# Two of eight experts multiplied in plain float32 in place of three split products

## The chip, the cores and the metric

The kernel runs on one core of a Trainium2 chip. The metric is the device time of one launch in microseconds. The median of three runs of the kernel before is 1239.47 us (1236.13 to 1243.42).

## The reference

Three stages follow one another: an attention over 4 x 12 heads of 448 tokens with 64 columns; a mixture of 8 experts over the 1792 tokens of 768 columns that come out of it, each token going to exactly one expert and each expert taking 224 tokens; and a dense layer with 2048 hidden columns.

```python
def _moe_ref(x, w_gate, w1, w2):
    logits = x @ w_gate
    order = np.argsort(-logits.flatten())
    for idx in order:                      # best (token, expert) pair first
        tok, e = idx // E, idx % E
        if assigned[tok] >= 0 or counts[e] >= cap: continue
        assigned[tok] = e; counts[e] += 1
    for e in range(E):
        mask = assigned == e
        h = np.maximum(x[mask] @ w1[e], 0.0)     # 224 x 768 by 768 x 1024
        out[mask] = h @ w2[e]                    # 224 x 1024 by 1024 x 768
def _moe2_ref(x, w_in, w_out):
    h = x @ w_in
    g = h * (1.0 / (1.0 + np.exp(-1.702 * h)))
    return g @ w_out
```

## The kernel before

After the attention (up to about 350 us of the span) the class `Moe` takes the experts in the order in which they fill up, two at a time (a pair): expert 0, expert 1, then the dense layer for their 448 tokens, and so on for four pairs. Weights come in chunks: an expert has 8 chunks of `w1` (768 x 128, 384 KB) and 6 of `w2` (1024 x 128, 512 KB), a pair of the dense layer 28 chunks.

A float32 product is made of three products in the reduced type `float32r`. `split` turns a chunk's tile `raw` into a high part `whi` (ScalarE, L966) and a low part `wlo` = raw - whi (L969: GpSimd for expert 0, in turn with VectorE for the later experts, by LO_VECTOR). The tokens are split in the same way: `xs` (L1022 and L1023), the hidden `hs` (L1061 and L1064), the output `zs` (L1061 and L1066). `mm3` (L1030 to L1032) then issues three products for each block of 128 x 128 weights: high by high, high by low, low by high. A block of an expert has 224 moving columns, one of the dense layer 448. A `w1` chunk has 6 blocks (18 products), a `w2` chunk 8 (24 products).

`ahead` keeps the chunks coming: up to 4 chunks loaded ahead and 2 split ahead. A `raw` buffer (there are 4) is free as soon as both parts are written.

`manual_schedule` leaves the instructions of each engine in the order in which the code issues them. After each chunk `back` issues other work with a budget: steps of the routing (`Route`), which finds the tokens of the next expert, and steps of `Convert`, which rewrites the dense layer's weights. The routing of expert 1 stands among the chunks of expert 0: 32 rank compares on VectorE (L568, L570, L574) write `B` and `Bd`, of which 8 and 16 buffers exist, and after each four of them TensorE sums them up (L591, L597) between two chunks; then come the counts (L605), a decision, sixteen one-hot rows `O` on VectorE (L642) with their products (L649), and the gather of expert 1's tokens by two GpSimd DMAs (L1007). During expert 1, GpSimd issues sixteen scatter DMAs (L694, tile `left`) that pack the remaining tokens; the routing of expert 2 starts on them. `Convert` steps run on ScalarE and VectorE (L886, L887, L900, L905), with loads `r` and stores `din` and `dout` on SyncE's queue, where the weight loads (L957) stand too.

Of the kernel before, what the change touches and what calls it, by code (L numbers as in the profile page):

```python
# [20 lines left out]
FT = mybir.dt.float32  # L21
# [4 lines left out]
AF = mybir.ActivationFunctionType  # L26
# [6 lines left out]
BESIDE = [3, 5, [(48, 1), (48, 3)]]  # L33
LO_VECTOR = [(0, 2, 4, 6, 8, 10, 12), (1, 3, 5, 7, 8, 11, 13)]
IDLE = (2, 4, 5)
GATE_A = (0, 4)
GATE_B = (2, 6)
PREP_AHEAD = (6, 5, 4, 2)
# [12 lines left out]
class Attn:  # L51
# [319 lines left out]
    def run(s, slot, beside):  # L371
# [27 lines left out]
        def gates(h, f, at):  # L399
            b, gs = divmod(h - 12, 12)  # L400
            for half in range(2):
                if b >= 0 and gs == at[half]:
                    f(b, half)
# [9 lines left out]
        for i in range(4):  # L413
# [7 lines left out]
            XP=lambda h: pairs(h, 5) and h < NHD - (5 < 7) and s.put_x((h - 5) // 2),  # L421
            GA=lambda h: gates(h, s.gate_a, GATE_A), GB=lambda h: gates(h, s.gate_b, GATE_B))
        for h in range(NHD):
# [496 lines left out]
class Moe:  # L920
# [20 lines left out]
    def load(s, n):  # L941
        kind, e, i = s.chunks[n]
        if kind in ("w1", "w2") and e not in s.reg:
            s.reg[e] = s.nc.sync.value_load(s.r.eid[0:1, e:e + 1], min_val=0, max_val=7)
        K = 6 if kind == "w1" or (kind == "w32" and i < 16) else 8
        t = s.pw.tile([128, 8, 128], FT, name="raw", bufs=4)[:, 0:K]
        if kind == "w32":
# [9 lines left out]
        s.nc.sync.dma_start(t, src)  # L957
        s.raw[n] = t

    def split(s, n):  # L960
        nc = s.nc
        t = s.raw.pop(n)
        K = t.shape[1]
        hi = s.pw.tile([128, 8, 128], FR, name="whi", bufs=3)[:, 0:K]
        lo = s.pw.tile([128, 8, 128], FR, name="wlo", bufs=3)[:, 0:K]
        nc.scalar.copy(hi, t)  # L966
        kind, e, i = s.chunks[n]
        eng = nc.vector if kind != "w32" and e > 0 and i + 8 * (kind == "w2") in LO_VECTOR[e % 2] else nc.gpsimd
        f = lambda: eng.tensor_tensor(lo, t, hi.bitcast(FT), op=OP.subtract)  # L969
        if eng is nc.vector:  # L970
            s.late[n] = f
        else:
            f()
        s.hl[n] = (hi, lo)

    def ahead(s):
        N = len(s.chunks)
        while s.nl < N and s.nl < s.used + s.LOAD:
            kind, e, _ = s.chunks[s.nl]
            if kind != "w32" and not s.r.done[e]:  # L980
                break
            if s.nl >= s.nsp + 4:
                break
            s.load(s.nl)
            s.nl += 1
        while s.nsp < s.nl and s.nsp < s.used + s.SPLIT:
            s.split(s.nsp)
            s.nsp += 1
# [23 lines left out]
    def xsplit(s, e, d):  # L1012

        nc = s.nc
        if d == 0:
            s.xs = s.pa.tile([128, 6, 2, 224], FR, name="xs", bufs=1)
        p = s.ps.tile([128, 2, 2, 112], FT, name="tr", bufs=2)
        for dd in range(2):
            for c in range(2):
                nc.tensor.transpose(p[:, dd, c], s.xg[:, c, (d + dd) * 128:(d + dd + 1) * 128], s.identf)  # L1020
        p = p.rearrange("p d c t -> p d (c t)")
        nc.scalar.copy(s.xs[:, d:d + 2, 0, :], p)  # L1022
        s.ev.append(lambda xs=s.xs: nc.vector.tensor_tensor(  # L1023
            xs[:, d:d + 2, 1, :], p, xs[:, d:d + 2, 0, :].bitcast(FT), op=OP.subtract))
# [9 lines left out]
    def expert(s, e, zs):  # L1034
        nc = s.nc
        s.low()
        xs = s.xs
        hs = s.pa.tile([128, 16, 2, 448], FR, name="gs", bufs=1)[:, 0:4].rearrange("p f h t -> p (f h t)")
        hs = hs.rearrange("p (f h t) -> p f h t", h=2, t=224)
        for f in range(8):  # L1040
            w = s.weights()
            p = s.ps.tile([128, 448], FT, name="mm", bufs=3)[:, 0:224]
            for d in range(6):
                s.mm3(p, w, d, (xs[:, d, 0], xs[:, d, 1]), d == 0, d == 5)
            s.ev.append(lambda f=f, p=p: s.parts(p, hs[:, f], AF.Relu))
            yield
        s.low()
        o = (e % 2) * 224
        for d in range(6):
            w = s.weights()  # L1050
            p = s.ps.tile([128, 448], FT, name="mm", bufs=3)[:, 0:224]
            for f in range(8):
                s.mm3(p, w, f, (hs[:, f, 0], hs[:, f, 1]), f == 0, f == 7)
            s.ev.append(lambda d=d, p=p: s.parts(p, zs[:, d, :, o:o + 224], AF.Copy))
            yield
        s.low()
# [116 lines left out]
    def run(s):  # L1173
# [13 lines left out]
        for pr in range(4):  # L1187
            zs = s.pa.tile([128, 6, 2, 448], FR, name="zs", bufs=1)
            for e in (2 * pr, 2 * pr + 1):
                early, done = None, 0  # L1190
                for n, _ in enumerate(s.expert(e, zs)):
# [11 lines left out]
                    if e == 0 and s.r.done[1]:  # L1203
# [3 lines left out]
                        elif n > early + 1 and done < 6:  # L1207
                            s.xsplit(1, done)
                            done += 2
                    s.back(0 if n == 7 else (3.1 if e == 0 else 1.4 if e == 1 else 0.6 if n < 8 else 1.2), True if e > 1 and n % 2 == 1 else None, e in IDLE and (e % 2 == 1 or bool(s.r.done[e + 1])))  # L1210
                if e == 0:
# [110 lines left out]
```

## Time and profile before

| | |
|---|---|
| median of three runs | 1239.47 us |
| the profiled execution | 1235.44 us, its span 1233.7 us |
| TensorE busy | 1147.0 us (93%) |
| VectorE, ScalarE, GpSimd busy | 768.1, 649.8, 695.6 us |
| first product of expert 0 | 376.87 us |
| first product of expert 1 | 444.71 us |
| first product of the dense layer, pair 0 | 494.07 us |

An engine's busy time includes the time in which an instruction has begun and waits for a memory port. A matmul's end is modelled, so the distance between the starts of two matmuls tells more than their durations. The granted clock of TensorE is given as a share of 2.4 GHz: 1.0 or 0.5 at a moment, and a mean over a stretch.

### The profile page before, as it was taken

What the parts mean: (1) busy time and instruction counts of PE and PEld (TensorE: products, weight loads), DVE (VectorE), ACT (ScalarE), POOL (GpSimd) and SP (SyncE); (2) the same over time, 40 slices, a digit from 0 to 9 for tenths busy, and PEclk for the clock granted to TensorE, in tenths of its full rate; (3) what the DMA queues carried; (4) which work ended last, traced back from release to release, by engine and by line L of the source; (5) the groups of instructions that cost most, each with busy time, mean ns of one, the idle gap of its engine ahead of it and who ended that gap; (6) DMA issues with size and microseconds to landing.
All of it is one profiled execution on the core that took longest, in us unless ns stands there. A gap on an engine that the chain in (4) does not pass through costs nothing.

```text
span 1233.7 us, 20534 instructions
## 1 busy us (share of the span) xinstructions
PE 1147.0 (93%) x7624; PEld 984.6 (80%) x7624; DVE 768.1 (62%) x1427; ACT 649.8 (53%) x1289; POOL 695.6 (56%) x591
## 2 busy tenths in 40 slices
PE   4899999999966887999999999999999999999995
PEld 3677767777535787888899988898998999999995
DVE  7699999999779766999754466455347303331100
ACT  4798889888642244765334454224544324444420
POOL 2688778883444476544645945545544565445552
PEclk9799999999957799999999999999999999999998
DMA  6455454523134277797647633437743345653421
GB/s 163 124 136 135 123 163 121 150 76 92 26 87 113 65 206 206 223 285 232 184 134 196 179 105 115 125 97 203 201 119 110 112 131 161 179 176 106 137 80 34
DMA packets 185508, 173.02 MB, mean 140 GB/s; under 512 B 9536, under 2 KB 159808, under 8 KB 185408
## 3 DMA queue, kind: packets, MB, share of 16 engines
q1 hardware_dynamic: 180080, 160.55, 45.6%
q0 software_dynamic: 4224, 11.14, 3.1%
q8 instruction: 60, 0.98, 0.3%
q14 instruction: 40, 0.33, 0.1%
q10 hardware_dynamic: 1104, 0.03, 0.1%
HBM read 147.96 MB, written 23.72 MB: 139 GB/s over the span
## 4 chain that ended last, share of the span: by engine, by line
PE 48%; DVE 8%; POOL 3%; DMA 2%; issue 1%; ACT 1%; POOLq 0%; ACTq 0%
PE mm L1030 15%; PE mm L1031 15%; PE mm L1032 15%; DMA xg<-xd,idx 2%; DVE B L568 2%; DVE B L570 1%; DVE wc L900 1%; DVE Bd L574 1%; POOL left L694 1%; PE tr L1099 1%; POOL wlo L969 1%; DVE wc L905 1%; PE tr L1020 1%; DVE gs L1078 1%; PE rc L591 1%
## 5 line engine op out<-in xcount | busy, mean ns | idle before, releaser
L969 POOL TENSOR_TENSOR wlo<-raw,whi 128x768 fp32r<-128x768 f32 (+1 forms) x175 | 371.0, 2122 | 369.6 <-ACT whi L966 358.9
L966 ACT CAST whi<-raw 128x768 fp32r<-128x768 f32 (+1 forms) x224 | 207.9, 928 | 181.4 <-issue 74.9
L1030 PE MATMUL mm<-gs,whi 128*128 128x224 f32 (+1 forms) x768 | 253.1, 330 | 1.2 <-DVE zs L1066 1.2
L1032 PE MATMUL mm<-gs,wlo 128*128 128x224 f32 (+1 forms) x768 | 248.7, 324 | 4.3 <-POOL wlo L969 4.3
L1031 PE MATMUL mm<-gs,whi 128*128 128x224 f32 (+1 forms) x768 | 248.7, 324 | 0.0
L1032 PEld LDWEIGHTS mm<-gs,wlo 128*128 128x128 f32 x768 | 148.5, 193 | 11.1 <-POOL wlo L969 4.8
L1030 PEld LDWEIGHTS mm<-gs,whi 128*128 128x128 f32 x768 | 148.6, 193 | 8.9 <-issue 1.5
L1031 PEld LDWEIGHTS mm<-gs,whi 128*128 128x128 f32 x768 | 148.6, 193 | 5.6
L1030 PE MATMUL mm<-zs,whi 128*128 128x448 f32 x384 | 143.6, 374 | 0.2 <-DVE zs L1066 0.2
L1032 PE MATMUL mm<-zs,wlo 128*128 128x448 f32 x384 | 141.1, 367 | 0.0
L1031 PE MATMUL mm<-zs,whi 128*128 128x448 f32 x384 | 141.0, 367 | 0.0
L239 ACT ACTIVATE A<-S,sm 112x448 f32<-112x448 f32 x192 | 122.6, 658 | 6.6 <-DVE sm L232 6.5
L232 DVE TENSOR_REDUCE sm<-S 112x2 f32<-112x896 f32 x96 | 104.2, 1086 | 21.2 <-PE S L221 20.1
L1030 PE MATMUL mm<-xs,whi 128*128 128x224 f32 x384 | 111.2, 290 | 6.1 <-DVE gs L1064 6.1
L1032 PE MATMUL mm<-xs,wlo 128*128 128x224 f32 x384 | 108.9, 284 | 4.2 <-POOL rspace L693 4.2
L1031 PE MATMUL mm<-xs,whi 128*128 128x224 f32 x384 | 109.7, 286 | 1.2 <-DVE xs L1023 1.1
L248 PE MATMUL pA<-ident,A 112*112 112x112 f32 x768 | 100.9, 266 | 2.5 <-DVE AT L257 2.2
L248 PEld LDWEIGHTS pA<-ident,A 112*112 112x112 f32 x768 | 84.9, 137 | 14.8 <-DVE AT L257 3.5
L969 DVE TENSOR_TENSOR wlo<-raw,whi 128x768 fp32r<-128x768 f32 (+1 forms) x49 | 61.1, 1246 | 55.3 <-ACT whi L966 55.2
L1076 ACT ACTIVATE mm<-mm 128x448 f32<-128x448 f32 x64 | 33.8, 528 | 113.0 <-PE mm L1032 113.0
L1030 PEld LDWEIGHTS mm<-xs,whi 128*128 128x128 f32 x384 | 77.5, 202 | 10.5 <-DVE gs L1064 7.6
L221 PE MATMUL S<-khi,qT 128*112 128x448 f32 x192 | 80.8, 421 | 4.4 <-ACT khi L209 4.4
(216 smaller groups left out, 2315.7 us busy)
## 6 DMA issues: line engine op xcount, KB each, us to landing
raw<-in_moe_w_dram SPq DMA_DIRECT2D x64, 384.0 KB
raw<-in_moe_w_dram SPq DMA_DIRECT2D x48, 512.0 KB
raw<-din SPq DMA_DIRECT2D x64, 384.0 KB
raw<-dout SPq DMA_DIRECT2D x48, 512.0 KB
r<-in_moe_w_in_dram SPq DMA_DIRECT2D x24, 512.0 KB
r<-in_moe_w_out_dram SPq DMA_DIRECT2D x24, 512.0 KB
din<-wc SPq DMA_DIRECT2D x24, 256.0 KB
dout<-wc SPq DMA_DIRECT2D x48, 128.0 KB
```

Source lines behind the costliest of these rows:

```text
L221: nc.tensor.matmul(p[:, c, 0:448], s.qT[h][:, i, :], mv.rearrange("p i t -> p (i t)"), start=(n == 0), stop=(n == 1))
L232: s.nc.vector.tensor_reduce(s.sums[h][:, 2 * u:2 * u + 2, 0], s.Sp[u][:, :, 0:448], axis=AX.X, op=OP.max, negate=True)
L239: s.nc.scalar.activation(s.A[h][:, i, :], p[:, c, 0:448], AF.Exp, bias=sm[:, i, 0:1], scale=1.0, accum_out=sm[:, i, 1:2])
L248: nc.tensor.transpose(p[:, qc], s.A[h][:, qc, kc * 112:(kc + 1) * 112], s.identf)
L568: V.tensor_scalar(b[:, 0:k], src[:, 0:k], sv, None, op0=OP.is_lt)
L570: V.tensor_scalar(b[:, k:], src[:, k:], sv, None, op0=OP.is_le)
L966: nc.scalar.copy(hi, t)
L969: f = lambda: eng.tensor_tensor(lo, t, hi.bitcast(FT), op=OP.subtract)
L1030: nc.tensor.matmul(p, hi[:, k], x[0], start=first, stop=False)
L1031: nc.tensor.matmul(p, hi[:, k], x[1], start=False, stop=False)
L1032: nc.tensor.matmul(p, lo[:, k], x[0], start=False, stop=last)
L1076: nc.scalar.activation(p, p, AF.Gelu_apprx_sigmoid)
```

## The change

For the experts in `FULL` (0 and 1) nothing is split. The loaded tile `raw` is itself the stationary operand, `xs` and `hs` are copied once in full float32, and one float32 product stands where three stood. The output `zs` is split as before, since the dense layer keeps its three products. As TensorE now reads `raw` itself, a buffer is free when the chunk's last product has run, and `ahead` loads one chunk less ahead while the chunk in use is such a one.

```diff
+FULL = (0, 1)
...
+    def whole(s, n):
+        kind, e, _ = s.chunks[n]
+        return kind != "w32" and e in FULL
...
     def split(s, n):
         t = s.raw.pop(n)
+        if s.whole(n):
+            s.hl[n] = t
+            return
...
-        while s.nl < N and s.nl < s.used + s.LOAD:
+        while s.nl < N and s.nl < s.used + s.LOAD - (s.used > 0 and s.whole(s.used - 1)):
...
+        if e in FULL:
+            nc.scalar.copy(s.xs[:, d:d + 2, 0, :].bitcast(FT), p)
+            return
         nc.scalar.copy(s.xs[:, d:d + 2, 0, :], p)
...
-                s.mm3(p, w, d, (xs[:, d, 0], xs[:, d, 1]), d == 0, d == 5)
-            s.ev.append(lambda f=f, p=p: s.parts(p, hs[:, f], AF.Relu))
+                if e in FULL:
+                    nc.tensor.matmul(p, w[:, d], xs[:, d, 0].bitcast(FT), start=d == 0, stop=d == 5)
+                else:
+                    s.mm3(p, w, d, (xs[:, d, 0], xs[:, d, 1]), d == 0, d == 5)
+            if e in FULL:
+                s.ev.append(lambda f=f, p=p: nc.scalar.activation(hs[:, f, 0].bitcast(FT), p, AF.Relu))
+            else:
+                s.ev.append(lambda f=f, p=p: s.parts(p, hs[:, f], AF.Relu))
...
-                s.mm3(p, w, f, (hs[:, f, 0], hs[:, f, 1]), f == 0, f == 7)
+                if e in FULL:
+                    nc.tensor.matmul(p, w[:, f], hs[:, f, 0].bitcast(FT), start=f == 0, stop=f == 7)
+                else:
+                    s.mm3(p, w, f, (hs[:, f, 0], hs[:, f, 1]), f == 0, f == 7)
```

On GpSimd's queue at the start of expert 1 there stand before the change, between the gather of its tokens (`xg`) and the scatter (`left`), low parts of weights:

```order
L1007 DMA xg<-xd,idx 112x768 x2
L969 TENSOR_TENSOR wlo<-raw,whi 128x1024
L969 TENSOR_TENSOR wlo<-raw,whi 128x768
L693 MEMSET rspace 1x1
L694 DMA left_157<-rec_68,pos 3584x10
```

and after it, from the last scatter to the next low part, which is the dense layer's:

```order
L694 MEMSET rspace 1x1
L695 DMA left_157<-rec_68,pos 3584x10
L978 TENSOR_TENSOR wlo<-raw,whi 128x768 x16
L978 TENSOR_TENSOR wlo<-raw,whi 128x1024 x7
L1016 DMA xg<-xd,idx 112x768 x2
```

The 28 low parts of experts 0 and 1 that stood on GpSimd and VectorE are gone, and the sixteen scatters follow one another.

On SyncE's queue, where the loads of expert 0 end, there stand before the change (`eid` is the number of the expert, `din` a store and `r` a load of `Convert`):

```order
L957 DMA raw<-in_moe_w_dram 128x8x128
L944 TENSOR_LOAD eid
L944 ISA x2
L957 ISA
L957 DMA raw<-in_moe_w_dram 128x6x128
L870 DMA din<-wc 128x4x128
L862 DMA r_5406<-in_moe_w_out_dram 128x2x512
```

and after it:

```order
L958 DMA raw<-in_moe_w_dram 128x8x128
L871 DMA din<-wc 128x4x128
L863 DMA r_5188<-in_moe_w_out_dram 128x2x512
L945 TENSOR_LOAD eid
L945 ISA x2
L958 ISA
L958 DMA raw<-in_moe_w_dram 128x6x128
```

The first load of expert 1 moved behind one store and one load of `Convert`.

## Rows read from the trace of the kernel before

**Rows 1.** Busy time by stretch; us, then each engine, clock, DMA share, GB/s.
```profile
377.00:441.00 64.00, 51.47 (x401) 45.85 (x400) 51.53 (x116) 18.31 (x31) 30.04 (x17) 0.79 0.35 100
441.00:494.00 53.00, 42.91 (x349) 41.12 (x347) 36.87 (x60) 25.37 (x47) 36.03 (x39) 0.94 0.71 202
500.00:560.00 60.00, 57.55 (x322) 50.10 (x321) 58.00 (x105) 41.54 (x72) 26.77 (x14) 0.97 0.85 265
```

**Rows 2.** Timeline of TensorE, stations: start us, us, line, tiles, idle before.
```profile
376.87 0.54 PE L1030 MATMUL mm<-xs,whi 128*128 128x224 f32 x1
...
389.95 0.27 PE L1032 MATMUL mm<-xs,wlo 128*128 128x224 f32 x1
...
390.71 0.37 PE L1030 MATMUL mm<-xs,whi 128*128 128x224 f32 x1
...
412.54 0.54 PE L591 MATMUL rc<-B,Cp 112*32 112x448 f16 x5 [0.98 <-DVE B L568]
...
414.34 0.53 PE L1030 MATMUL mm<-xs,whi 128*128 128x224 f32 x1
...
444.71 0.35 PE L1030 MATMUL mm<-xs,whi 128*128 128x224 f32 x1
...
474.68 0.37 PE L1032 MATMUL mm<-gs,wlo 128*128 128x224 f32 x1 [3.57 <-POOL wlo L969]
...
494.07 0.47 PE L1030 MATMUL mm<-zs,whi 128*128 128x448 f32 x1 [0.21 <-DVE zs L1066]
```

**Rows 3.** Timeline of VectorE and GpSimd during the routing of expert 1.
```profile
360.77 3.09 DVE L642 TENSOR_SCALAR O<-iota,acc 112x224 f16<-112x224 f16 x16
...
367.79 3.58 POOL L969 TENSOR_TENSOR wlo<-raw,whi 128x768 fp32r<-128x768 f32 x2
...
369.22 2.23 DVE L568 TENSOR_SCALAR B<-vr,v 112x112 f16<-112x112 f32 x1 [2.27 <-ACT vr L549]
...
386.11 4.25 DVE L568 TENSOR_SCALAR B<-vr,v 112x896 f16<-112x896 f32 x7
...
401.25 0.26 DVE L568 TENSOR_SCALAR B<-vr,v 112x112 f16<-112x112 f32 x1
...
402.22 0.33 DVE L568 TENSOR_SCALAR B<-vr,v 112x224 f16<-112x224 f32 x1
...
423.46 7.18 DVE L642 TENSOR_SCALAR O<-iota,acc 112x224 f16<-112x224 f16 x16
```

**Rows 4.** Timeline of TensorE, split products of expert 0, at two clocks.
```profile
431.66 0.41 PE L1030 MATMUL mm<-gs,whi 128*128 128x224 f32 x1
431.87 0.41 PE L1031 MATMUL mm<-gs,whi 128*128 128x224 f32 x1
...
434.16 0.27 PE L1030 MATMUL mm<-gs,whi 128*128 128x224 f32 x1
...
437.73 0.27 PE L1032 MATMUL mm<-gs,wlo 128*128 128x224 f32 x1
```

**Rows 5.** Timeline of TensorE, plain float32 products of the attention, 448 columns.
```profile
49.49 0.55 PE L268 MATMUL av<-AT,vt 112*64 112x448 f32 x2
49.87 0.55 PE L268 MATMUL av<-AT,vt 112*64 112x448 f32 x2
50.24 0.55 PE L268 MATMUL av<-AT,vt 112*64 112x448 f32 x2
```

**Rows 6.** Timeline of ScalarE before the first compare.
```profile
367.87 0.83 ACT L966 CAST whi<-raw 128x768 fp32r<-128x768 f32 x1 [1.43 <-DMA raw<-in_moe_w_dram]
368.60 0.53 ACT L549 COPY vr<-rv 112x448 f32<-112x448 f32 x1
```

**Rows 7.** Expert 1: SyncE's weight loads, a ScalarE wait for one, and DMA share.
```profile
450.63 6.63 SPq L957 DMA_DIRECT2D raw<-in_moe_w_dram  x3
...
455.56 0.83 ACT L966 CAST whi<-raw 128x768 fp32r<-128x768 f32 x1 [2.69 <-DMA raw<-in_moe_w_dram]
...
460.00:470.00 10.00, 8.67 (x71) 8.49 (x71) 4.44 (x7) 5.63 (x10) 8.76 (x13) 0.93 0.91 250
```

## The prediction

> **What bounds the kernel now.** I read the busy times by stretch first. The change touches only 377 to 494 us, the experts 0 and 1. There TensorE is busy for 51.47 of 64 and 42.91 of 53 us, at a mean clock of 0.79 and 0.94 [rows 1]. The next stretch, the dense layer of pair 0, has TensorE busy for 57.55 of 60 us at 0.97: it is bound by TensorE, and what is saved ahead of it should move it as a block. So the question is what the stretch of experts 0 and 1 waits for.
>
> Second, the pace of the products. Split products with 224 columns start 0.111 us apart at full clock (33 of them stand from 434.16 to 437.73) and 0.21 at half (431.66, 431.87) [rows 4]. The 576 products of the two experts, at 0.111, are 64 us; the stretch from the first of them to the dense layer takes 494.07 - 376.87 = 117.2 us [rows 2]. The other 53 us are the routing's own small products, waits, and half clock.
>
> Third, the waits. In expert 0 the routing on VectorE is late, since GpSimd's low parts hold it up: a compare of 112 columns that takes 0.26 us at 401.25 takes 2.23 us at 369.22, until the two low parts that began at 367.79 are through; sixteen one-hot rows take 3.09 us before any low part runs, and 7.18 us with them [rows 3]. TensorE's queue holds the rank products between the chunks, so each such stall stops it too, and after it the clock is at half. In expert 1 TensorE waits for a low part directly, for instance 3.57 us ahead of 474.68 [rows 2].
>
> **The change part by part.** *TensorE's products get dearer.* A float32 product of the attention runs as two instructions. Those on the same half of the array start at 49.49, 49.87 and 50.24, 0.375 us apart for 448 columns at full clock [rows 5]; by columns that is 0.188 us for 224, more than the 0.111 that a split product takes, load included. A block then takes 2 x 0.188 = 0.375 us where three products took 0.333. That is 0.042 more for each of 192 blocks, +8.1 us if nothing else changed. A `w1` chunk is 6 blocks = 2.25 us, a `w2` chunk 8 blocks = 3.0 us.
>
> The Trainium skill has two rules for this product. FP8 and Floating Point Precision (TensorE Precision Notes) gives true float32 four passes through the array, with which the 0.375 agrees. Perfetto Trace Analysis (Engine Utilization, first note) halves the array's output rate for FP32_LOW_HIGH, which would make it two passes; that is the third rival below.
>
> *Splits go.* 28 high parts on ScalarE, 28 low parts on GpSimd and VectorE, the low parts of `xs` and `hs`. These lie beside TensorE and count only where it waits, so I walk from station to station.
>
> Start of expert 0. The copy `vr` waited for a high part, which ended about 368.7 (367.87 + 0.83) [rows 6]; without it the compares start some 2 us sooner, and the first is not stalled for 2 us. The first product waits for the tokens, whose gather is not changed; only the low part of `xs` falls away: 376.2, estimated, for 376.87.
>
> Chunks 0 to 6. Seven chunks are 15.8 us; a first stretch at half clock costs 1.3 (my estimate); between two chunks the rank products take from 389.95 to 390.71 less one step, 0.65 us [rows 2], six times 3.9. Chunk 6 ends at 397.2. VectorE could do its 32 compares sooner, at 0.61 (4.25 / 7) for a plain one and 0.97 (401.25 to 402.22) for one with its diagonal [rows 3], but 8 buffers hold it back: the last eight, of the dearer sort, can begin after chunk 4, about 391.8, and take 7.8 us: 399.6. So TensorE still waits here, 2.4 us. The tail of the ranking with the counts was 412.54 to 414.34, 1.8 us: chunk 7 starts at 401.4 where it was 414.34, **13 us sooner** [rows 2].
>
> Rest of expert 0: one `w1` and six `w2` chunks 20.3, one-hot products 3.2 (paced by 3.09 us of VectorE), small products and transposes 1.5, and half clock after the two pauses, which I put at 3.4 (between 0 and 7). That is 28.4: expert 1 starts at 429.8 for 444.71, **15 us sooner**. A move on SyncE lies here: expert 1's first load now stands behind a store that waits for VectorE. VectorE is through with it about 418, and a load that was issued about 451 landed by 455.6 [rows 7], 5 us: 424, before 429.8. Nothing waits.
>
> Expert 1: 36.0 us of chunks, 1.2 of transposes for the routing, 1.0 of rank products. The scatter on GpSimd begins about 419 and runs without low parts between: the routing has its data before the transposes come. New here is the wait of a load for the *end* of a chunk: it has three chunks, 6.8 us, to land, against those 5. The loads of this expert, the first of the next and `Convert`'s come to about 9 MB in 37 us, 250 GB/s, what the DMA queues moved at a share of 0.91 [rows 7]. I add 3 us (0 to 7). Pair 0 starts at 429.8 + 41.2 = 471.0 for 494.07: **23 us sooner**.
>
> *Pair 0 and later.* Instructions and order are the same, TensorE is the bound, VectorE's backlog is smaller: no change.
>
> Sum: 1235.44 - 23 = 1212.4 for an execution like the profiled one (span 1233.7). The median of the runs is 4.0 above that one, so I forecast **1216 us**. The open sizes (half clock 0 to 7 for 3.4, DMA 0 to 7 for 3, the first product) make it 1209 to 1223.
>
> **The rivals.** *Loads pace expert 1.* If a load takes 9 us instead of 5 under the denser traffic, each chunk lasts 3 us and more, and expert 1 is some 10 us longer: 1226. For it speaks the share of 0.91 and the shorter lead, against it that 250 GB/s is not the most that was moved (265 over 60 us at 0.85 in rows 1).
>
> *Pair 0 gives it back.* VectorE is busy for 58.00 of 60 us there [rows 1]. If that is `Convert` pacing the dense layer's chunks, an earlier start only means waits for them, about a third of the gain: 1224. Against it: TensorE is as busy, and VectorE comes in with less left to do.
>
> *Float32 needs two passes.* Then the load of the weights is the limit, about 0.111 us an instruction, a block 0.222 us, 29 us less on TensorE for both experts. Expert 0 would wait for the compares, expert 1 for 32 us of loads; of the 29 about 17 remain: 1199. The 0.375 of rows 5 speaks against it.
>
> *Slower: the clock stays at half.* The float32 block takes 0.75 us at half clock, 0.375 more. My sum has some 4.7 us of that loss. From about 62 more blocks of the 192 on the 23 us are gone; if all of expert 0 and half of expert 1 ran so, the loss would be 54 us less 4.7 already counted: 1265. Before, half clock followed each pause of TensorE; the pauses become fewer, and the clock was full while the attention ran its float32 products at 49.49. So it is unlikely.
>
> *Nothing moves*: if the routing's chain through VectorE had its length for another reason than GpSimd. The twins in rows 3 speak against it.
>
> **How the numbers follow.** Forecast 0.70; loads 0.12; pair 0 0.07; two passes 0.04; half clock 0.04; nothing 0.03. 1216 is the likeliest case. The range 1206 to 1228 takes in its own bounds with 3 us for the spread of the runs, and the two cases in which part is given back; about 0.15 are left out. A measurement here can tell some 0.5%, 6 us, from no change: faster than 1233.3 are the forecast and nearly all of the cases with a smaller gain, 0.91; within 0.5% 0.04; slower 0.05.
>
> **What the profile after would show.** Right: two instructions to a block, 0.188 us apart; compares without 2 us stalls; chunk 7 near 401, expert 1 near 430, pair 0 near 471, and from there the same distances as before. Wrong: a step far from 0.188; TensorE idle for DMA `raw` in expert 1; pair 0 longer than before; a mean clock below 0.8 between 377 and 430.

## The result and the profile after

The changed kernel took 1219.91 us (median of 4 runs, 1217.41 to 1221.09), the kernel before beside it 1239.38 (1236.13 to 1243.42). The ratio is 0.9843, its 95% interval 0.9815 to 0.9871: 19.5 us faster. Forecast were 1216 us and 1206 to 1228. The profiled execution took 1219.52 us. Its page begins (busy us, share of the span, instructions)

```profile
span 1217.7 us, 20040 instructions
...
PE 1146.2 (94%) x7432; PEld 982.7 (81%) x7432; DVE 722.8 (59%) x1398; ACT 626.0 (51%) x1261; POOL 646.6 (53%) x570
```

TensorE is busy for as long as before (1147.0 us), VectorE and GpSimd for 45 and 49 us less. So nearly all of the 16.0 us by which the span shrank is time in which TensorE waited; the dearer products (8.1 us by the prediction's sum) and the shorter time at half clock must about cancel.

Busy time by stretch comes first (columns as in [rows 1]). The stretches are cut where expert 0, expert 1 and the dense layer of pair 0 now begin or run.

```profile
377.00:426.00 49.00, 47.87 (x336) 42.23 (x336) 28.45 (x95) 7.49 (x19) 7.15 (x14) 0.98 0.55 152
426.00:478.00 52.00, 43.47 (x219) 40.29 (x218) 15.34 (x42) 13.67 (x32) 15.05 (x23) 0.90 0.65 186
480.00:540.00 60.00, 57.54 (x307) 49.81 (x306) 56.59 (x94) 39.80 (x68) 26.84 (x14) 0.94 0.85 255
```

Expert 0 keeps TensorE busy for 47.87 of 49 us at a clock of 0.98, where it was 51.47 of 64 at 0.79 [rows 1]. Expert 1 does not look like that: 8.5 us of 52 are idle and the clock is 0.90. Pair 0 is what it was, 57.54 of 60 for 57.55.

The stations on TensorE's timeline (start, us, line, tiles, idle time before), to be laid beside [rows 2]:

```profile
375.57 4.32 PE L1057 MATMUL mm<-xs,raw 128*128 128x224 f32 x12
...
395.21 2.54 PE L1057 MATMUL mm<-xs,raw 128*128 128x224 f32 x12
...
399.89 0.54 PE L592 MATMUL rc<-B,Cp 112*32 112x448 f16 x5 [0.68 <-DVE B L569]
...
401.52 1.76 PE L1057 MATMUL mm<-xs,raw 128*128 128x224 f32 x8
...
425.94 0.94 PE L1057 MATMUL mm<-xs,raw 128*128 128x224 f32 x4
428.18 1.02 PE L1057 MATMUL mm<-xs,raw 128*128 128x224 f32 x4 [1.31 <-issue]
432.45 7.98 PE L1057 MATMUL mm<-xs,raw 128*128 128x224 f32 x28 [3.25 <-issue]
442.95 6.63 PE L1057 MATMUL mm<-xs,raw 128*128 128x224 f32 x24 [2.52 <-ACT gs L1061]
451.04 7.05 PE L1057 MATMUL mm<-xs,raw 128*128 128x224 f32 x36 [1.45 <-DMA raw<-in_moe_w_dram]
...
477.88 0.47 PE L1042 MATMUL mm<-zs,whi 128*128 128x448 f32 x1
```

Chunk 7 of expert 0 starts at 401.52 (was 414.34), expert 1 at 425.94 (444.71), pair 0 at 477.88 (494.07). So 18.8 us had been won when expert 1 began, and 16.2 when it ended: expert 1 took 51.9 us, more than the 49.4 of before. From pair 0 to the end of the span it is 739.8 us for 739.6.

VectorE's compares and one-hot rows in 377 to 441 us (line, operation, shape, count; busy us, mean ns of one; idle before):

```profile
L569 DVE TENSOR_SCALAR B<-vr,v 112x896 f16<-112x896 f32 x9 | 5.6, 682 | 5.8 <-PE rc L592 5.8
L571 DVE TENSOR_SCALAR B<-vr,v 112x896 f16<-112x896 f32 x8 | 4.9, 682 | 1.0 <-issue 0.6 <-PE rc L592 0.4
L643 DVE TENSOR_SCALAR O<-iota,acc 112x224 f16<-112x224 f16 x16 | 3.2, 272 | 0.5 <-PE rc L650 0.5
```

No compare is stalled: the widest take 0.68 us each, and the sixteen rows `O` 3.2 us, where 7.18 were needed [rows 3]. What VectorE waits for now is a free buffer `B`, that is, TensorE.

The four waits of TensorE in expert 1 were not in the forecast. ScalarE's timeline there shows what stands behind them:

```profile
427.60 0.53 ACT L1032 COPY xs<-tr 128x448 f32<-128x448 f32 x1 [4.42 <-PE tr L1029]
428.02 0.61 ACT L1082 ACTIVATE zs<-mm 128x224 fp32r<-128x224 f32 x2
431.87 0.53 ACT L1032 COPY xs<-tr 128x448 f32<-128x448 f32 x1 [3.23 <-remote]
...
442.55 0.85 ACT L1061 ACTIVATE gs<-mm 128x224 f32<-128x224 f32 x3 [9.03 <-remote]
```

The transposes that fill `tr` had all ended at 426.10. The copies of them ran at 427.60 and 431.87. The last products of chunks 0 to 2 of expert 1 ended about 434, 438 and 440 us; all three evictions ran together at 442.55. "remote" says that the trace has no instruction that ended when the awaited semaphore was counted up: the awaited one, on TensorE, had ended 2 to 8 us before. The trace also records when each semaphore was counted up: TensorE's at 427.57 and 431.85, and then not before 442.46, each time just before the copy or the evictions ran. A product's end is modelled, so it stays open whether the count alone was late or the writing of the result too. SyncE waited for the same counts, since a weight buffer is free when TensorE's last product on it is through:

```profile
425.43 17.42 SPq L958 DMA_DIRECT2D raw<-in_moe_w_dram  x2
442.89 0.54 SPq L871 DMA_DIRECT2D din<-wc  x1
```

Two loads fill 17.42 us of its queue; the second left at 442.48. All this falls together with GpSimd's sixteen scatters, most of which stand 1.25 us apart, from 419.70 to 440.04:

```profile
419.70 0.97 POOL L695 DMA_INDIRECT left<-rec,pos  x1 [4.73 <-DVE pos L689]
420.67 0.09 POOL L694 MEMSET rspace<- 1x1 f32 x1
420.97 0.95 POOL L695 DMA_INDIRECT left<-rec,pos  x1 [0.22 <-issue]
```

Two readings of this were open: the loads are too few ahead for chunks of 2.3 us, or the counts of TensorE come late beside the scatters and hold up evictions and loads alike.

### The profile page after: what moved, and what is told of

Read it like the earlier page. It is cut to its first block, busy times and chain, and to the rows that moved or that the text cites. A ratio compares the mean times of both kernels' runs of the same rounds, so it can differ in the third digit from the quotient of the medians.

```text
span 1217.7 us, 20040 instructions
## 1 busy us (share of the span) xinstructions
PE 1146.2 (94%) x7432; PEld 982.7 (81%) x7432; DVE 722.8 (59%) x1398; ACT 626.0 (51%) x1261; POOL 646.6 (53%) x570
## 4 chain that ended last, share of the span: by engine, by line
PE 78%; DVE 13%; DMA 2%; ACT 2%; issue 2%; POOL 1%; another core or an unknown queue 1%; POOLq 0%; SPq 0%; DVEq 0%; ACTq 0%
PE mm L1042 16%; PE mm L1043 15%; PE mm L1044 15%; PE S L222 7%; PE av L269 6%; PE pA L249 5%; PE mm L1072 3%; DVE wc L901 2%; PE mm L1057 2%; DMA xg<-xd,idx 2%; DVE B L569 2%; PE tp L188 1%; PE tp L203 1%; DVE B L571 1%
## 5 line engine op out<-in xcount | busy, mean ns | idle before, releaser
L978 POOL TENSOR_TENSOR wlo<-raw,whi 128x768 fp32r<-128x768 f32 (+1 forms) x154 | 324.9, 2111 | 354.5 <-ACT whi L975 351.2
L975 ACT CAST whi<-raw 128x768 fp32r<-128x768 f32 (+1 forms) x196 | 182.0, 928 | 137.0 <-issue 44.3
L1042 PE MATMUL mm<-gs,whi 128*128 128x448 f32 (+1 forms) x672 | 224.2, 334 | 0.0
L1043 PE MATMUL mm<-gs,whi 128*128 128x448 f32 (+1 forms) x672 | 220.4, 328 | 0.0
L1044 PE MATMUL mm<-gs,wlo 128*128 128x448 f32 (+1 forms) x672 | 220.3, 328 | 0.0
L1042 PEld LDWEIGHTS mm<-gs,whi 128*128 128x128 f32 x672 | 128.1, 191 | 7.4 <-issue 1.5
L1044 PEld LDWEIGHTS mm<-gs,wlo 128*128 128x128 f32 x672 | 128.2, 191 | 6.4 <-POOL wlo L978 0.2
L1043 PEld LDWEIGHTS mm<-gs,whi 128*128 128x128 f32 x672 | 128.3, 191 | 5.5
L269 PE MATMUL av<-AT,vt 112*64 112x448 f32 x384 | 82.5, 552 | 0.0
L978 DVE TENSOR_TENSOR wlo<-raw,whi 128x768 fp32r<-128x768 f32 (+1 forms) x42 | 51.2, 1219 | 50.8 <-ACT whi L975 50.8
L1042 PEld LDWEIGHTS mm<-zs,whi 128*128 128x128 f32 x384 | 73.0, 190 | 9.9 <-issue 3.8
L1099 DVE TENSOR_TENSOR gs<-mm,gs 128x448 fp32r<-128x448 f32 x64 | 39.5, 619 | 69.7 <-ACT gs L1098 69.6
L1042 PE MATMUL mm<-xs,whi 128*128 128x224 f32 x288 | 80.0, 278 | 0.9 <-DVE gs L1085 0.9
```

Of the source, the lines that this page charges most:

```text
L269: nc.tensor.matmul(p[hh * 64:(hh + 1) * 64, :], s.grp[g]["v"][:, hl, kc * 64:(kc + 1) * 64], s.AT[h][:, kc, :], start=(kc == 0), stop=(kc ...
L1042: nc.tensor.matmul(p, hi[:, k], x[0], start=first, stop=False)
L1043: nc.tensor.matmul(p, hi[:, k], x[1], start=False, stop=False)
L1044: nc.tensor.matmul(p, lo[:, k], x[0], start=False, stop=last)
L1099: s.ev.append(lambda f=f, p=p: nc.vector.tensor_tensor(gs[:, f, 1], p, gs[:, f, 0].bitcast(FT), op=OP.subtract))
```

## The experiments

**One expert at a time.** `FULL = (0, 1)` becomes `(0,)` and `(1,)`.

> Expert 0 alone in whole float32; expert 1 is split again as in the kernel before. Theory (the gain is VectorE, which GpSimd's low parts no longer stall; the loss in expert 1 is GpSimd's 16 scatters without a break, beside which TensorE's semaphore counts arrive late): expert 0 as in the changed kernel, expert 1 starts at 426, plus or minus 2; expert 1's low parts break up the scatters again, so expert 1 takes 46 to 50 us, as the 49.4 of before, pair 0 starts at 472 to 476, and the time is 1214 to 1220 us, no worse than the changed kernel. Rival (each expert saves its half by having one product in place of three): 1229 to 1231 us.

> Expert 1 alone in whole float32; expert 0 is split as in the kernel before. Theory (as for the run with expert 0 alone): expert 0 as in the kernel before, expert 1 starts at 445, plus or minus 2; expert 1 takes 48 to 53 us with the scatters in one unbroken run, so pair 0 starts at 493 to 498 and the time is 1233 to 1243 us: nothing gained. Rival (each expert saves its half): 1229 to 1231 us.

Expert 0 alone gave 1220.07 us, ratio 0.9844 (0.9804 to 0.9883); expert 1 alone 1225.01, ratio 0.9880 (0.9838 to 0.9923); before was 1237.85. The two gains, 17.8 and 12.8 us, add up to 30.6, near the 30.0 that both experts gave in the run `after_again` below. For expert 0 the time is at the top of the theory's range and expert 1 starts at 426.13 as expected, but it takes 51.3 us, not 46 to 50, and pair 0 starts at 477.40, not by 476: TensorE waits 2.0, 3.0 and 1.9 us there for GpSimd, where the low parts of expert 1 stand among the scatters. With expert 1 alone both sides missed: I had forecast nothing, the rival half of 19.5. Its 96 float32 blocks ran without a pause beside 16 scatters in one unbroken run (441.34 to 461.90):

```profile
446.88 18.34 PE L1057 MATMUL mm<-xs,raw 128*128 128x224 f32 x96
465.69 6.29 PE L1072 MATMUL mm<-gs,raw 128*128 128x224 f32 x32 [0.48 <-ACT gs L1061]
...
485.73 0.47 PE L1042 MATMUL mm<-zs,whi 128*128 128x448 f32 x1
```

Expert 1 took 38.8 us here, with the same lead of loads and the same scatters as in the trace above where it took 51.9. The short lead of loads falls as a cause by this run. The scatters alone were not enough either; no count came late in expert 1 of this trace.

**No scatters.** The sixteen scatters become one copy (the compaction is left out).

```diff
+        if n == 16:
+            nc.sync.dma_start(s.left[n2][0:112 * n2, :].rearrange("(p j) c -> p j c", j=n2), s.rec[:, 0:n2, :])
+        else:
```

> The changed kernel, with the 16 indirect stores of the first compaction of tokens replaced by one plain copy of the first 12 columns (the compaction is left out, so later experts route other tokens; shapes and all other work are the same). Theory (the scatters hold back TensorE's semaphore counts, by which evictions and weight loads start): evictions of expert 1's first chunks follow their products within 1 us, weight loads start as buffers come free, expert 1 takes 41 to 44 us in place of 51.9, pair 0 starts at 467 to 470 and the time is 1208 to 1213 us. Rival (a lead of three weight loads is too short for float32 chunks of 2.3 us, whatever GpSimd does): expert 1 still takes 49 us or more, time 1217 to 1221 us.

1214.65 us, ratio 0.9793 (0.9748 to 0.9839). The time is a little above the 1208 to 1213 expected. Expert 1 took 39.6 us and pair 0 started at 465.0, both sooner than expected, but the run does not tell the two readings apart: the session was one in which counts were in time beside unbroken scatters too (`one_alone` above, `no_low_part` below). A run without scatters in a session with late counts is lacking. The total also moved by something else. Without the scatters the routing of expert 2 is issued sooner, TensorE's queue holds its products earlier, and the first half of pair 0 (465.0 to 544.1) took 79.1 us where it takes 67 to 72 in the other runs; TensorE waited there for VectorE's compares and one-hot rows, 7.1 us in all.

**Three products, no low part.** In the kernel before, experts 0 and 1 read the high part in place of the low part, which is not made.

```diff
+        if kind != "w32" and e < 2:
+            s.hl[n] = (hi, hi)
+            return
```

> The kernel before, with three products for a block throughout, but the low parts of the weights of experts 0 and 1 are not computed: the products with the low part read the high part once more (a part of the computation of experts 0 and 1 is replaced). Theory (GpSimd's low parts stalled VectorE's compares; the number of products has little to do with the gain): expert 0's compares run unstalled, the wait after its chunk 6 ends at 399 to 403, expert 1 starts at 420 to 428 in place of 444.71; expert 1 meets the unbroken scatters and takes 45 to 53 us; time 1212 to 1222 us. Rival (the gain comes from one product in place of three): expert 1 starts after 436 and the time is 1230 us or more.

1209.49 us, ratio 0.9764 (0.9725 to 0.9803): with all three products left, the gain is there, 28.4 us. Expert 1 starts at 424.3, as the theory had it; it takes 41.2 us, not 45 to 53 (no count came late in this trace), and the time is below the 1212 to 1222 expected. So one product in place of three is not where the time goes; the absent low parts are.

**Low parts that nobody needs.** The changed kernel, with GpSimd's subtractions of before put back, into a tile that is never read.

```diff
         if s.whole(n):
             s.hl[n] = t
+            kind, e, i = s.chunks[n]
+            if not (e > 0 and i + 8 * (kind == "w2") in LO_VECTOR[e % 2]):
+                d = s.spare[:, 0:K]
+                nc.gpsimd.tensor_tensor(d, t, d, op=OP.subtract)
             return
```

> The changed kernel, with a subtraction on GpSimd for each chunk of experts 0 and 1 whose low part GpSimd made in the kernel before: same size, from the loaded weights into a spare tile that nobody reads, so nothing waits for it but the reuse of the weight buffer. Theory (GpSimd's work as such stalls VectorE's compares, and TensorE waits for these): compares that last 0.68 us stretch to 2 to 4 us again, the wait after expert 0's chunk 6 ends at 406 to 413 in place of 398.5, expert 1 starts at 433 to 445 in place of 424.6, the time is 10 to 20 us above the changed kernel's on the same chip. Rival (before, TensorE waited for the low parts themselves, not for VectorE): expert 1 starts at 424 to 427 and the time is within 3 us of the changed kernel's.

1231.73 us (10 runs), 14.1 above the changed kernel in the same session (1217.59). Expert 1 starts at 446.0, 1 us later than the top of what was expected and 20.9 later than in `after_third`, a run of the changed kernel beside it. The time grows by less, since expert 1 takes 45.1 us, without a late count, for 50.8 there. The timelines of VectorE, GpSimd and TensorE:

```profile
385.28 11.06 DVE L571 TENSOR_SCALAR B<-vr,v 112x896 f16<-112x896 f32 x8
396.27 2.36 DVE L569 TENSOR_SCALAR B<-vr,v 112x112 f16<-112x112 f32 x1
...
399.09 2.41 DVE L575 SCALAR_TENSOR_TENSOR Bd<-vr,v,before 112x112 f16<-112x112 f32 x1
```

```profile
382.15 19.22 POOL L977 TENSOR_TENSOR spare<-raw,spare 128x768 f32<-128x768 f32 x6 [8.36 <-DMA raw<-in_moe_w_dram]
```

```profile
410.13 0.91 PE L592 MATMUL rc<-B,Cp 112*32 112x448 f16 x5 [2.65 <-DVE B L569]
...
412.57 1.84 PE L1063 MATMUL mm<-xs,raw 128*128 128x224 f32 x4
```

Eight compares take 11.06 us in place of 4.9; one of 112 columns takes 2.36 us, much as the stalled one in [rows 3], while six subtractions fill GpSimd. Chunk 7 is back at 412.57. Nothing waits for these subtractions' results, and ahead of expert 1 TensorE's waits are for VectorE's compares (8.1 us) and one-hot rows (2.4), none for a load. So in expert 0 it is GpSimd's work as such, through VectorE, that held TensorE. This agrees with the Trainium skill, SBUF — State Buffer (SBUF: two separate sides), by which VectorE and GpSimd share a pair of ports that one of them holds for a whole instruction.

**The kernels once more.** No edit. A session below is a set of runs made one after the other on the same chip.

> The changed kernel as it is, once more, since in its first trace TensorE's semaphore counts arrived 2 to 8 us late beside GpSimd's scatters, while in the runs with expert 1 alone and with no low part, beside the same unbroken scatters, they did not. Theory A (late counts belong to that execution or chip): expert 1 takes 39 to 42 us, pair 0 starts at 464 to 468 in place of 477.88, the time is 1205 to 1211 us. Theory B (late counts come with the combination of both experts in float32 and the scatters): expert 1 takes 49 us or more again, and the time is 1217 to 1222 us.

> The kernel before as it is, for its trace on the chip of the other runs. Theory A: no count of TensorE's semaphore comes late beside the scatters, so the pause of 3.6 us at 471 is gone or shorter; pair 0 starts at 488 to 494. Theory B: the trace is as it was, with pair 0 at 494.

> The changed kernel as it is, a third time, to stand beside the two runs below on the same chip. Where no count of TensorE's semaphore is late: 1203 to 1209 us, expert 1 39 to 40 us. Where counts are late beside the scatters, as in its first trace: 1217 to 1221 us, expert 1 about 52 us.

> The changed kernel beside the one with the wide spacer, to see the two on another chip. Where TensorE's counts are in time: 1204 to 1210 us. Where they are late: 1215 to 1221 us, with ScalarE waiting 3 us and more in expert 1 for counts of products that had ended.

| session | before, us | changed, us | expert 1 of the changed kernel, us | longest ScalarE wait there for a late count, us |
|---|---|---|---|---|
| the result | 1239.38 | 1219.91 | 51.9 | 9.0 |
| `after_again` | 1237.28 | 1207.30 | 39.2 | none |
| `after_third` | 1238.44 | 1217.59 | 50.8 | 11.2 |
| `after_fourth` | 1234.76 | 1213.45 | 47.8 | 6.7 |

`after_again` and `after_third` took the times expected for counts in time and for late counts; `after_fourth`, with late counts, took less than the 1215 to 1221 expected for them. In `after_again` (ratio 0.9747, 0.9687 to 0.9806) TensorE, ScalarE and the stretches of expert 1 read so:

```profile
424.60 11.53 PE L1057 MATMUL mm<-xs,raw 128*128 128x224 f32 x60
436.45 7.05 PE L1057 MATMUL mm<-xs,raw 128*128 128x224 f32 x36 [0.32 <-DMA raw<-in_moe_w_dram]
443.74 6.29 PE L1072 MATMUL mm<-gs,raw 128*128 128x224 f32 x32 [0.24 <-DMA raw<-in_moe_w_dram]
```

```profile
427.71 0.35 ACT L1061 ACTIVATE gs<-mm 128x224 f32<-128x224 f32 x1
429.36 0.36 ACT L1061 ACTIVATE gs<-mm 128x224 f32<-128x224 f32 x1 [1.29 <-PE mm L1057]
431.63 0.36 ACT L1061 ACTIVATE gs<-mm 128x224 f32<-128x224 f32 x1 [1.91 <-PE mm L1057]
```

```profile
425.00:464.00 39.00, 38.44 (x216) 37.15 (x215) 15.44 (x42) 13.33 (x31) 15.03 (x23) 1.00 0.91 251
...
430.00:442.00 12.00, 11.68 (x62) 11.36 (x61) 0.69 (x1) 4.13 (x9) 7.24 (x15) 1.00 1.04 279
```

Each eviction follows its product, and loads flow at a DMA share of 1.04 from 430 to 442. In the trace of the result the same stretch reads

```profile
430.00:442.00 12.00, 7.98 (x28) 7.20 (x28) 2.38 (x4) 1.65 (x3) 8.52 (x15) 0.72 0.04 5
```

that is, a share of 0.04: no load was issued; after 442 they follow one another closely and TensorE waits for one (`raw`, 1.45 us). GpSimd's scatters stand 1.25 us apart in both. So the late counts go with the session, not with the kernel alone. Nor do they go with the chip alone: `one_alone` and `no_low_part`, beside unbroken scatters and without a late count, ran on the chip of `after_fourth`. And not every kernel of such a session shows them: `idle_low`, whose subtractions stand among the scatters, has none in expert 1 in the session of `after_third`. One more thing goes with the session: in every trace of the three with late counts, 13 to 21 of TensorE's counts are missing from the record, and counts of the other engines too; in the seven traces of the other two sessions none is. Whether the recording has a part in the delay, no run shows.

The kernel before does not pay for the late counts: it took 1237 to 1239 us in sessions of either kind (1234.76 in the last), though its first trace too has one ScalarE wait of 3.3 us for such a count. And in `before_again` (1238.81), where no count was late, the pause of 3.6 us at 471 [rows 2] stays, since TensorE waits for a low part there. So for `before_again` theory A held for the counts and for pair 0 (491.7), but not for the pause.

**Scatters further apart.** The memset between two scatters grows from 1x1 to 112x768.

```diff
-            nc.gpsimd.memset(s.spacer, 0.0)
+            nc.gpsimd.memset(s.wide if n == 16 else s.spacer, 0.0)
```

> The changed kernel, with the 1x1 memset between the scatters of the first compaction made 112x768, so that the scatters stand further apart. Where counts are late on this chip, theory (they are late because scatter follows scatter): the delays fall below 1 us and the time to 1206 to 1212 us; rival (they do not depend on the distance): 1217 to 1221 us. Where none is late: the same as the changed kernel within 3 us, as expert 2's routing has over 100 us in hand.

> The wide spacer once more. Theory (it only takes away the late counts): where they are late, 6 to 12 us below the changed kernel; where they are in time, within 3 us of it, at 1204 to 1212 us. Rival (GpSimd's longer stretch of scatters costs something of its own, by the later load of the packed tokens or by memsets that hold up VectorE): where counts are in time, 3 to 6 us above the changed kernel.

In the session of `after_third` it gave 1209.25 us, 8.3 below the changed kernel (its ratio to before is 0.9769, 0.9722 to 0.9817; the changed kernel's 0.9831, 0.9788 to 0.9875); in that of `after_fourth` 1210.11, 3.3 below (0.9781, 0.9750 to 0.9813, against 0.9821, 0.9790 to 0.9853), less than the 6 expected. The intervals overlap in both sessions, but the runs do not: the slowest with the wide spacer (1212.06 and 1210.63) is below the fastest without (1214.97 and 1212.33). What the traces show is plainer: with the scatters 1.87 us apart, ScalarE never waits for a late count in expert 1, in two sessions in which the changed kernel did for 11.2 and 6.7 us. GpSimd and TensorE in `wide_spacer`:

```profile
420.70 0.75 POOL L695 MEMSET rwide<- 112x768 f32 x1
421.62 0.96 POOL L696 DMA_INDIRECT left<-rec,pos  x1 [0.17 <-issue]
```

```profile
425.96 18.54 PE L1058 MATMUL mm<-xs,raw 128*128 128x224 f32 x96
...
459.53 0.81 PE L1073 MATMUL mm<-gs,raw 128*128 128x224 f32 x3 [2.59 <-DMA raw<-in_moe_w_dram]
```

The 96 instructions run without a pause. Some of the gain is lost later: TensorE waits 1.98 us for the routing of expert 2, whose tokens come after the longer run of scatters, and 2.59 us for a load; expert 1 takes 43.4 us, and 45.4 in `wide_again`, not 39.2. So the version was faster than the changed kernel in both sessions with late counts. It was not tried in one without them, so the rival of `wide_again` (a cost of its own where counts are in time) stays untested.

**Experts 2 and 3 as well.** `FULL = (0, 1, 2, 3)`.

> Experts 2 and 3 in whole float32 too, where TensorE is the bound and all else waits for it. Theory (a float32 block takes 0.378 us and three products 0.333, 96 blocks an expert): expert 2 and 3 each 3 to 5 us longer than in the changed kernel, the time 6 to 10 us above its time on the same chip. Rival (the pace of float32 is hidden, or the freed VectorE and ScalarE take away as much): within 3 us of the changed kernel.

1213.84 us, 6.5 above the changed kernel in the same session. Expert 2 went from 37.3 to 39.5 us, expert 3 from 32.6 to 36.6. Where TensorE is the bound, the dearer product costs what the forecast's step said (0.042 us for each of 96 blocks, 4.0 an expert). Expert 2 pays 2.2: in the changed kernel TensorE waited 1.3 us for VectorE there, here not at all.

## Why the prediction was right, and where it was not

- **The pace of float32.** Forecast 0.188 us an instruction; 60 in 11.53 us start 0.189 apart, and 0.199 in expert 0's `w1` chunks (12 in 2.54), where the first step is longer. The two instructions follow the float32 rows of the attention [rows 5] to 1%: the rival with two passes does not hold here. By columns each instruction takes nearly twice as long as a split product (0.375 us for 448 columns; split products of 448 start 0.21 apart at 478), so a halved rate fits one instruction, and a float32 product is two of them.
- **VectorE's stalls.** Right, and now shown: `no_low_part` takes the low parts away and leaves the products (28.4 us gained), `idle_low` brings GpSimd's low parts back without a reader (14.1 lost of the 20.9 that the changed kernel gained beside it).
- **Expert 0.** First product 375.57 (forecast 376.2), end of chunk 6 397.75 (397.2), chunk 7 401.52 (401.4). The rest of expert 0 was mis-sized: 28.4 us forecast, 24.4 measured. The 3.4 us for half clock after the pauses did not come (clock 0.98 from 377 to 426), and the one-hot products took 2.0 for 3.2. Expert 1 began at 425.94 for 429.8, 18.8 us sooner than before where 15 were forecast.
- **Expert 1.** The step that failed: 41.2 us forecast, 51.9 measured. The sum put nothing for the time between a product's end and the eviction or load that waits for it; it was 2 to 8 us. The 3 us that I added for DMA and the rival "loads pace expert 1" looked at the right buffers for the wrong reason. Where counts are in time, expert 1 takes 39.2 us at a share of 0.91 and waits 0.56 us for loads. In the run of the result TensorE's counts came late beside the scatters, and evictions and loads started late with them. I had noted that the scatters would run without low parts between, and took it for harmless.
- **Pair 0 and later.** Right: 57.54 of 60 busy, 739.8 us to the end for 739.6. VectorE's 58.00 of 60 did not make it give the gain back.
- **The sum.** Pair 0 at 477.88 for 471.0 is 6.9 us too early; the 4.0 us from the profiled execution to the median were not needed (0.4 after) and covered over half of it. So 1216 is near 1219.91 partly by luck: two errors of opposite sign and an allowance. In a session without late counts the same kernel takes 1207.3, at the low end of the range.
- **Half clock.** The mean clock of expert 1 fell to 0.90, after the pauses and with them; in the session without these it was 1.00. The rival that the clock stays at half has nothing for it.

## What to carry to other kernels

Work that is off the critical path on one engine can hold another by a shared resource: read the duration of the same instruction with and without a neighbour before counting its work as hidden, and test it with work that nobody reads. When such work goes, look at what now follows what on its engine: the low parts had also kept the scatters apart. And where a buffer comes free by TensorE's count in place of ScalarE's, everything that delays that count delays the loads.

## What the runs showed of the hardware

- In three of the five sessions (the result's, `after_third`'s, `after_fourth`'s) TensorE's semaphore counts became visible 2 to 10 us after the products had ended, while GpSimd issued indirect DMAs 1.25 us apart; in the other two, with the same sequence on GpSimd, at once. At 1.87 us apart no ScalarE wait for a late count was left. That the scatters cause the delay is argued from these distances, and what differs between sessions is open.
- One float32 product for 224 columns (0.378 us) costs little more than three `float32r` products (0.333 us, 0.111 each), so whole float32 is cheap where the splitting, not TensorE, is in the way.
